# Small results, maxima and conversion words of attention in PSUM, and row sums in four groups

## The chip, the core and the metric

One core of a Trainium2 chip runs the whole program. The metric is the device time of one execution in microseconds (us), as the median of several runs. The engines are TensorE (PE, with its weight loads as PEld), VectorE (DVE), ScalarE (ACT), GpSimd (POOL) and the DMA queues, which SyncE (SP) feeds for the most part. Each engine takes its instructions in the order in which they were written and waits on semaphores for what the others produce.

## What is computed

The reference runs three stages. Attention comes first: queries are averaged in pairs, so that 576 queries meet 1152 keys in each of 4 x 8 heads.

```python
q_pool = q.reshape(B, H, S // factor, factor, D).mean(axis=3)
scores = scale * np.matmul(q_pool, k.transpose(0, 1, 3, 2))
scores = scores - np.max(scores, axis=-1, keepdims=True)
attn = np.exp(scores)
attn = attn / (np.sum(attn, axis=-1, keepdims=True) + 1e-09)
return np.matmul(attn, v).astype(np.float32)
```

The 2304 rows that come out then go through a mixture of 8 experts, where each row takes the expert with the largest gate value, and through one dense feed-forward layer with a softplus. The change touches attention and the gate computation that rides along with it; the expert and feed-forward stages keep their code.

## The kernel before, in words

**Tiling.** `attention` (from L17) handles two heads at once, a pair p, and there are 16 pairs, four in each batch b. A pair has two halves of 288 queries, and a half has nine chunks of 128 keys. A step g is one chunk of one half, so there are 288 steps, counted as `NG`. In step g, `smat` (L168) lets PE compute the scores of the next chunk into a PSUM tile `st` with eight matmuls (L175), `ex` (L176) lets ACT exponentiate them into the SBUF tile `P` (L178), `pv` (L213) lets PE multiply P with v (L218), and `add` (L180) sums P over chunks into tiles `acc`, from which row sums are made.

**Row maxima.** The maximum that is taken off the scores has to be known before `smat` runs on that pair, so a separate pass goes ahead of it. `srow` (L109) computes 384 scores of 128 queries with two matmuls (L118) into a PSUM tile named `sr`, and DVE reduces them to one column (L119). There are 27 such rows for a pair and 432 in all. After the last row of a pair `mfin` (L121) reduces the columns to one maximum (L128, tile `nm`), splits it into two halves of 16 bits (`nh`) and lets PE transpose it into place (L145). For pairs 0 and 1 the split is made by DVE (L130, L131); for the later pairs by two ACT instructions and one on POOL (L135 to L137).

**Row sums.** `GS` (L341) puts the nine chunks in three groups of three. Each group needs two additions, 128 x 576 in f32. They run on POOL (L192), except for chunk 4 of pairs 1 to 13 and chunks 2, 5 and 8 of pair 14, which the table `DVA` (L344) gives to DVE (L190). `rsum` (L194) then sums over the partitions with PE: four matmuls of 288 columns for the first two groups (L203) and four of 144 for the third (L208), each of which the trace shows as two; it stands three steps after the last chunk of its half (`RSD`).

**The gate.** After the last pair of a batch `lstage` (L223) runs once for each half, over batches 0 to 2 with the flag `port`. It divides by the row sums, makes the logits, finds the expert of each row, its gate value and its rank among the rows of that expert, writes the rows of x to DRAM (`xt`, L295) and one-hot rows `OHID` (L332). It is a chain of some 30 short instructions of DVE, with six on POOL among them (L268, L283, L287, L291, L326, L327). The table `LSTEPS` (L338) gives each piece its step after the end of the half.

**Conversions.** Twelve tiles of a later weight arrive as 64-bit words and are turned into f32 by three DVE instructions each (`convert`, L998; L1007, L1008, L1009) while attention runs. The loop from L372 gives each of the three a step of its own, the least busy by an estimate.

**The PSUM tiles `sr`.** The pool `srp` (L36) has three of them, used in turn. Rows of maxima, transposes, row sums and gate matmuls all draw from it, 533 times in attention. A tile can be written again only when the reader of its last use has finished, so PE gets at most three such tiles ahead of the engine that empties them.

**The order.** The loop at L441 writes the instructions out by hand, step by step: `smat` of the next chunk, the copy of a finished half out of PSUM, the exponential, the pieces that tables or `best` (L356) put into this step alternating with rows of maxima, then `pv`, and last the additions. The number of rows by step is set by `rows` (L351).

Of the kernel before, what the change touches and what calls it, by code (L numbers as in the profile page):

```python
# [12 lines left out]
B,H,S,D=4,8,1152,64  # L13
# [3 lines left out]
def attention(ctx,late,tc,I,C,x_dram,LG,gate,fill,early):  # L17
# [12 lines left out]
    accp=ctx.enter_context(tc.tile_pool(name="acc",bufs=4)); ssp=ctx.enter_context(tc.tile_pool(name="ss",bufs=7))  # L30
# [3 lines left out]
    xsp=ctx.enter_context(tc.tile_pool(name="xs",bufs=3))  # L34
# [3 lines left out]
    exp_=srp  # L38
# [82 lines left out]
    def mfin(p,ta=0,tb=9):  # L121
# [37 lines left out]
        return [a]+([a2] if p>=2 else [])+[b,c(0),c(1)]+([d(0),d(1)] if ta==0 else [])  # L159
# [63 lines left out]
    def lstage(b,half,last=False):  # L223
        port=b<B-1; G=nc.gpsimd
# [50 lines left out]
        def ff():  # L275
            V.tensor_reduce(out=T('f',[96,3]),in_=z['eq'],axis=AX.X,op=ALU.min)
# [4 lines left out]
        def ra():  # L281
            V.tensor_reduce(out=T('os',[96,8]),in_=OH.rearrange("p t e -> p e t"),axis=AX.X,op=ALU.add)
            (G if port else V).tensor_tensor(out=C['RS'][:,st+1],in0=C['RS'][:,st],in1=z['os'],op=ALU.add)  # L283
        def ga():
            V.tensor_reduce(out=g,in_=z['ed'],axis=AX.X,op=ALU.add)
        def gb():
            (G if port else V).tensor_scalar(out=g,in0=g,scalar1=1e-9,scalar2=1.0/SX,op0=ALU.add,op1=ALU.mult)  # L287
        def gc():
            V.reciprocal(out=g,in_=g)
        def gd():  # L290
            if last or port: (G if port else V).tensor_tensor(out=z['r'].rearrange("p (t a) h -> p t (a h)",t=3),in0=z['r'].rearrange("p (t a) h -> p t (a h)",t=3),in1=e3(g),op=ALU.mult)  # L291
# [25 lines left out]
        def cm():  # L317
            if last or port: V.tensor_tensor(out=T('cm',[96,3,17]),in0=RK.unsqueeze(2).to_broadcast([96,3,17]),in1=C['iota128'][:96,1:18].unsqueeze(1).to_broadcast([96,3,17]),op=ALU.is_ge)
# [5 lines left out]
        def rp():  # L324
            if port:
                G.tensor_scalar(out=T('rp',[96,3]),in0=RB,scalar1=-128.0,scalar2=None,op0=ALU.mult)  # L326
                G.tensor_tensor(out=z['rp'],in0=z['rp'],in1=RK,op=ALU.add)  # L327
            else: V.scalar_tensor_tensor(out=T('rp',[96,3]),in0=RB,scalar=-128.0,in1=RK,op0=ALU.mult,op1=ALU.add)
        def oi(j):
# [130 lines left out]
    def tail(E,nx):  # L460
# [8 lines left out]
        xs=[xsp.tile([96,512],F32,name="xs") for j in range(3)]  # L469
# [472 lines left out]
def tile_kernel(ctx,tc,I,out):  # L942
    nc=tc.nc
    if True:
      c1=ExitStack(); late=ExitStack(); mst=ExitStack(); P={}
      with tc.manual_schedule():
# [9 lines left out]
        if True:  # L956
# [109 lines left out]
```

## Time and profile before

| what | value |
|---|---|
| median of 3 runs | 1131.71 us (1131.65 to 1132.65) |
| the profiled execution | 1132.7 us, of which the span takes 1130.9 us |
| busy in the span | PE 94%, PEld 62%, DVE 75%, ACT 57%, POOL 43% |
| attention, first to last exponential | from 22.9 us to some 488 us |
| longest groups | DVE L119 225.8 us, ACT L178 185.4 us, PE L218 173.7 us |

Attention is followed by the experts (to about 740 us) and the dense layer. In attention all four engines are busy most of the time, while POOL does little afterwards; a share of the whole span therefore says little, and stretches have to be read one by one. A matmul's busy time is modelled and overlaps with its neighbours'. "Idle before" of an instruction is the engine's idle time ahead of it, and behind the arrow stands the instruction that ended it.

### The profile page before, as it was taken

Reading aid. Unit: us, or ns where it says so; the run is one execution under the profiler, and the core shown is the slowest. Engines: PE = TensorE matmul, PEld = TensorE weight load, DVE = VectorE, ACT = ScalarE, POOL = GpSimd, SP = SyncE. Lnnn points to the kernel's source line nnn. Section 1 sums busy time; section 2 is a strip of 40 time slices with the busy share of each in tenths; the row PEclk is TensorE's granted clock in tenths of the full one; section 3 lists DMA queues with packets and bytes.
Section 4 is the critical chain, followed back from the end, with each engine's and each line's share of the span. In section 5 each row is a group of like instructions: output and inputs, shape, how many; then the busy total and the mean of one; then the engine's idle time right before and its main releaser. Section 6 shows DMA issues by size and latency. Waiting matters only on the chain. (4 is left out here: it accounts for less than half of the span.)

```text
span 1130.9 us, 23702 instructions
## 1 busy us (share of the span) xinstructions
PE 1057.6 (94%) x9423; PEld 706.6 (62%) x9423; DVE 846.1 (75%) x1461; ACT 646.1 (57%) x1136; POOL 491.8 (43%) x414
## 2 busy tenths in 40 slices
PE   5798989999999999998989998999999999999996
PEld 2566756776677666677777777885444444446662
DVE  5867678868886788989798887749867676767762
ACT  5566756776677665657555665646544444444441
POOL 7788867988898885633333222200000100100100
PEclk9999999999999999999999999999999999999999
DMA  9343417441764151426678887731101000000100
GB/s 254 80 106 94 123 47 196 138 123 42 190 148 112 32 154 41 168 86 223 239 254 281 292 274 248 236 112 29 47 1 28 38 1 19 38 1 11 38 10 30
DMA packets 42949, 129.64 MB, mean 115 GB/s; under 512 B 5841, under 2 KB 12881, under 8 KB 40914
## 3 DMA queue, kind: packets, MB, share of 16 engines
q1 hardware_dynamic: 39794, 118.12, 34.9%
q0 software_dynamic: 3040, 9.96, 2.5%
q8 instruction: 76, 1.25, 0.5%
q14 instruction: 39, 0.32, 0.1%
HBM read 108.13 MB, written 20.45 MB: 114 GB/s over the span
## 5 line engine op out<-in xcount | busy, mean ns | idle before, releaser
L119 DVE TENSOR_REDUCE mx<-sr 128x1 f32<-128x384 f32 x432 | 225.8, 550 | 103.9 <-PE sr L118 99.8
L178 ACT ACTIVATE P<-st 128x576 f32<-128x576 f32 x288 | 185.4, 650 | 124.6 <-PE st L175 112.3
L810 POOL DMA_INDIRECT out_dram<-io,CIDS x18 | 21.6, 1198 | 357.0 <-ACT io L808 311.1
L218 PE MATMUL pv<-P,v 128*64 128x288 f32 x1152 | 173.7, 415 | 0.9 <-ACT P L178 0.7
L175 PE MATMUL st<-Q,KB 128*64 128x288 f16 x1152 | 159.2, 289 | 1.9 <-ACT Q L157 1.9
L175 PE MATMUL st<-Q,KA 128*64 128x288 f16 x1152 | 160.0, 290 | 0.0
L118 PE MATMUL sr<-KA,Q 128*64 128x384 f16 x864 | 134.2, 340 | 19.2 <-ACT KA L90 8.3
L192 POOL TENSOR_TENSOR acc<-acc,P 128x576 f32<-128x576 f32 x88 | 124.7, 1417 | 28.8 <-DVE acc L190 22.4
L662 ACT ACTIVATE mhl<-mraw 128x512 f16<-128x512 f32 x160 | 98.1, 625 | 55.3 <-DMA mraw<-in_wm_dram 27.5
L627 PE MATMUL l<-xf,wl 128*128 128x256 f16 (+1 forms) x384 | 125.1, 326 | 0.0
L625 PE MATMUL l<-xf,WIH 128*128 128x256 f16 (+1 forms) x384 | 125.1, 326 | 0.0
L626 PE MATMUL l<-xf,WIH 128*128 128x256 f16 (+1 forms) x384 | 125.1, 326 | 0.0
L667 DVE SCALAR_TENSOR_TENSOR mhl<-mraw,mhl 128x512 f16<-128x512 f32 x140 | 98.7, 725 | 26.2 <-ACT mhl L662 25.5
L192 POOL TENSOR_TENSOR acc<-P 128x576 f32<-128x576 f32 x70 | 100.8, 1440 | 22.1 <-ACT P L178 21.0
L801 PE MATMUL o<-WOH,g 128*128 128x512 f16 x288 | 109.1, 379 | 1.2 <-ACT io L808 0.7
L803 PE MATMUL o<-WOH,g 128*128 128x512 f16 x288 | 109.1, 379 | 0.0
L802 PE MATMUL o<-wl,g 128*128 128x512 f16 x288 | 109.1, 379 | 0.0
L218 PEld LDWEIGHTS pv<-P,v 128*64 128x64 f32 x1152 | 85.9, 139 | 34.8 <-ACT P L178 5.7
L784 ACT ACTIVATE e<-e 128x1024 f32<-128x1024 f32 x36 | 38.0, 1057 | 101.2 <-DVE m L782 101.2
L175 PEld LDWEIGHTS <-KB 128*64 128x64 f16 x1152 | 73.3, 111 | 25.5 <-issue 2.9
L175 PEld LDWEIGHTS <-KA 128*64 128x64 f16 x1152 | 72.9, 111 | 24.0 <-issue 7.1
L626 PE MATMUL l<-hT,mhl 128*128 128x256 f16 x288 | 79.2, 275 | 7.1 <-DVE hT L694 7.1
(256 smaller groups left out, 2240.7 us busy)
## 6 DMA issues: line engine op xcount, KB each, us to landing
mraw<-in_wm_dram SPq DMA_DIRECT2D x80, 512.0 KB, 4.6
kr<-in_k_dram SPq DMA_DIRECT2D x30, 576.0 KB, 9.7
qr<-in_q_dram SPq DMA_DIRECT2D x16, 576.0 KB, 5.9
v<-in_v_dram SPq DMA_DIRECT2D x16, 576.0 KB, 4.3
mraw<-in_w_out_dram SPq DMA_DIRECT2D x16, 512.0 KB, 4.3
stg<-in_w_in_dram SPq DMA_DIRECT2D x12, 512.0 KB, 5.8
y_dram<-w SPq DMA_DIRECT2D x20, 256.0 KB, 4.6
xs_dram<-xs SPq DMA_DIRECT2D x24, 192.0 KB, 2.1
```

The source lines that it names most:

```text
L118: nc.tensor.matmul(sr[64*i:64*i+64,:KW],lhsT=q[:,hh,0,r:r+64],rhs=ka[:,hh,k0:k0+KW],start=True,stop=True)
L119: nc.vector.tensor_reduce(out=MX[p][:,t,kh:kh+1],in_=sr[:,:KW],axis=AX.X,op=ALU.max,negate=True)
L175: nc.tensor.matmul(st[o:o+64,h,:HQ],lhsT=w[:,h,c*128+o:c*128+o+64],rhs=q[:,h,i,qs],start=(i==0),stop=(i==1))
L178: nc.scalar.activation(out=P[g],in_=ST.pop(g)[:,:,:HQ],func=ACTF.Exp,scale=1.0/16)
L192: nc.gpsimd.tensor_tensor(out=A,in0=B_,in1=P[g],op=ALU.add)
L218: nc.tensor.matmul(t[64*h:64*h+64,:HQ],lhsT=V[p][:,c,64*h:64*h+64],rhs=P[g][:,h],start=(c==0),stop=(c==NCH-1))
L625: nc.tensor.matmul(o,lhsT=wh_,rhs=x[0],start=first,stop=False)
L626: nc.tensor.matmul(o,lhsT=wh_,rhs=x[1],start=False,stop=False)
L627: nc.tensor.matmul(o,lhsT=wl_,rhs=x[0],start=False,stop=last)
L801: nc.tensor.matmul(o,lhsT=g[:,0,i,cs],rhs=WOH[:,fc],start=(fc==0),stop=False)
L802: nc.tensor.matmul(o,lhsT=g[:,0,i,cs],rhs=WOL(fc),start=False,stop=False)
L803: nc.tensor.matmul(o,lhsT=g[:,1,i,cs],rhs=WOH[:,fc],start=False,stop=(fc==15))
```

## The change

Row sums are made from four groups of chunks, (0,1), (2,3), (4,5) and (6,7,8). That is five additions for a half instead of six. `DVA` keeps pair 14 alone, so that DVE makes four additions in the whole program instead of 32, and POOL 156 instead of 158. `rsum` has an even number of groups, and so it makes eight matmuls of 288 columns and none of 144. The pool `acc` gets a fifth tile, and `xs` loses its third.

Every pair now splits its maximum on DVE, with `nm` in an `sr` tile. In `lstage` the small intermediates are written to `sr` tiles, the six POOL instructions move to DVE, three reductions are made a second time so that one copy lies in PSUM, and the three one-hot rows are written to one `sr` tile that ACT copies out. The three DVE instructions of a conversion stand directly behind each other, and the first two write an `sr` tile. Three small instructions of the setup go from DVE to POOL. In all the `sr` pool is used 610 times: 17 more for maxima, 12 for conversions and 48 for the gate. `LSTEPS` has new steps.

```diff
-    accp=ctx.enter_context(tc.tile_pool(name="acc",bufs=4)); ssp=ctx.enter_context(tc.tile_pool(name="ss",bufs=7))
+    accp=ctx.enter_context(tc.tile_pool(name="acc",bufs=5)); ssp=ctx.enter_context(tc.tile_pool(name="ss",bufs=7))
...
-    xsp=ctx.enter_context(tc.tile_pool(name="xs",bufs=3))
+    xsp=ctx.enter_context(tc.tile_pool(name="xs",bufs=2))
...
-            st['nm']=smp.tile([128,9],F32,name="nm"); st['nh']=smp.tile([128,9,2],F16,name="nh")
-            nm,nh=st['nm'][:,:n],st['nh'][:,:n]
+
+            st['nh']=smp.tile([128,9,2],F16,name="nh")
+            nm,nh=srp.tile([128,512],F32,name="sr")[:,:n],st['nh'][:,:n]
             nc.vector.tensor_reduce(out=nm,in_=MX[p][:,ta:tb],axis=AX.X,op=ALU.min)
-            if p>=2: return
...
+        def ps(*w): return srp.tile([96,512],F32,name="sr")[:,:w[-1]]
...
             if port:
-                V.tensor_tensor(out=T('d',[96,3,8]),in0=lg,in1=e3(z['m']),op=ALU.is_equal)
-                G.tensor_tensor(out=T('eq',[96,3,8]),in0=z['d'],in1=C['iotaE8'].unsqueeze(1).to_broadcast([96,3,8]),op=ALU.mult)
+
+                w=ps(32); d=w[:,8:32].rearrange("p (t e) -> p t e",t=3)
+                V.tensor_reduce(out=w[:,0:3],in_=lg,axis=AX.X,op=ALU.min)
+                V.tensor_tensor(out=d,in0=lg,in1=e3(w[:,0:3]),op=ALU.is_equal)
+                V.tensor_tensor(out=T('eq',[96,3,8]),in0=d,in1=C['iotaE8'].unsqueeze(1).to_broadcast([96,3,8]),op=ALU.mult)
...
+        def o3():
+            w=srp.tile([96,512],F32,name="sr")[:,:384].rearrange("p (t w) -> p t w",t=3)
+            for j in range(3):
+                V.tensor_scalar(out=w[:,j],in0=C['iota'][:96],scalar1=z['rp'][:,j:j+1],scalar2=C['idc'][:,t0+j:t0+j+1],op0=ALU.is_equal,op1=ALU.mult)
+            nc.scalar.copy(out=C['OHID'][:,t0:t0+3],in_=w)
...
-    NG=NPAIR*18; GS=((0,1,2),(3,4,5),(6,7,8)); GL=((0,1,2,3),(4,5,6),(7,),(8,)); GK=((0,1),(2,3),(4,5),(6,7,8)); ET=238; TS=(1,1,2,4,3); TX=(11,13); RSD=3; LD=2
+    NG=NPAIR*18; GS=((0,1),(2,3),(4,5),(6,7,8)); GL=((0,1,2,3),(4,5,6),(7,),(8,)); GK=((0,1),(2,3),(4,5),(6,7,8)); ET=238; TS=(1,1,2,4,3); TX=(11,13); RSD=3; LD=2
...
-    DVA={**{p:(4,) for p in range(1,14)},14:(2,5,8),15:()}
+    DVA={14:(2,5,8),15:()}
...
-                def b(): nc.vector.tensor_scalar(out=dst,in0=z['s'][:,:,1],scalar1=3,scalar2=0x3FFFFFF8,op0=ALU.logical_shift_left,op1=ALU.bitwise_and)
-                def c(): nc.vector.scalar_tensor_tensor(out=dst,in0=z['s'][:,:,1],scalar=-0x40000000,in1=dst,op0=ALU.bitwise_and,op1=ALU.bitwise_or)
-                def d(): nc.vector.scalar_tensor_tensor(out=dst,in0=z['s'][:,:,0],scalar=29,in1=dst,op0=ALU.logical_shift_right,op1=ALU.bitwise_or)
-                return a,b,c,d
...
+                def c(): nc.vector.scalar_tensor_tensor(out=w(),in0=z['s'][:,:,1],scalar=-0x40000000,in1=w(),op0=ALU.bitwise_and,op1=ALU.bitwise_or)
+                def d(): nc.vector.scalar_tensor_tensor(out=dst,in0=z['s'][:,:,0],scalar=29,in1=w(),op0=ALU.logical_shift_right,op1=ALU.bitwise_or)
+                def bcd(): b(); c(); d()
+                return (a,bcd) if name=="stg" else (a,b,c,d)
...
-                nc.vector.tensor_tensor(out=bias,in0=mf[:,0].unsqueeze(2).to_broadcast([96,24,8]),in1=bb[:,0].unsqueeze(1).to_broadcast([96,24,8]),op=ALU.mult)
+                nc.gpsimd.tensor_tensor(out=bias,in0=mf[:,0].unsqueeze(2).to_broadcast([96,24,8]),in1=bb[:,0].unsqueeze(1).to_broadcast([96,24,8]),op=ALU.mult)
```

On DVE, around the first conversion (`stg` holds the raw words, `w_0_70` the finished tile, `mx` the columns of maxima), there stood before:

```order
L119 TENSOR_REDUCE mx<-sr 128x1 x9
L1007 TENSOR_SCALAR w_0_70<-stg 128x512
L119 TENSOR_REDUCE mx<-sr 128x1 x5
L1008 SCALAR_TENSOR_TENSOR w_0_70<-stg,w_0_70 128x512
L190 TENSOR_TENSOR acc<-P 128x576
L119 TENSOR_REDUCE mx<-sr 128x1 x5
L1009 SCALAR_TENSOR_TENSOR w_0_70<-stg,w_0_70 128x512
```

And now:

```order
L130 TENSOR_SCALAR nh<-sr 128x9
L131 SCALAR_TENSOR_TENSOR nh<-sr,nh 128x9
L119 TENSOR_REDUCE mx<-sr 128x1 x11
L1024 TENSOR_SCALAR sr<-stg 128x512
L1025 SCALAR_TENSOR_TENSOR sr<-stg,sr 128x512
L1026 SCALAR_TENSOR_TENSOR w_0_70<-stg,sr 128x512
L119 TENSOR_REDUCE mx<-sr 128x1 x11
```

The three pieces came together with no row of maxima between them, the addition on DVE is gone, and the split of the maximum is here.

On DVE, in the first half of the gate of batch 0 (`LG` logits, `m` their best, `d` and `eq` the search for the expert, `OH` its one-hot rows), there stood before:

```order
L267 TENSOR_TENSOR d<-LG,m 96x24
L119 TENSOR_REDUCE mx<-sr 128x1
L1009 SCALAR_TENSOR_TENSOR w_1_71<-stg,w_1_71 128x512
L119 TENSOR_REDUCE mx<-sr 128x1 x3
L285 TENSOR_REDUCE gate<-ed 96x3
L276 TENSOR_REDUCE f<-eq 96x3
L119 TENSOR_REDUCE mx<-sr 128x1
L278 TENSOR_TENSOR OH<-cc,f 96x24
```

And now:

```order
L264 TENSOR_REDUCE sr<-LG 96x3
L265 TENSOR_TENSOR sr<-LG,sr 96x24
L266 TENSOR_TENSOR eq<-sr,cc 96x24
L119 TENSOR_REDUCE mx<-sr 128x1 x3
L275 TENSOR_REDUCE sr<-eq 96x3
L277 TENSOR_TENSOR OH<-cc,sr 96x24
L119 TENSOR_REDUCE mx<-sr 128x1
L286 TENSOR_REDUCE sr<-ed 96x3
L288 TENSOR_SCALAR gate<-sr 96x3
```

The product `eq` came over from POOL, `OH` stands directly behind its minimum, and each short result passes through an `sr` tile of its own.

On PE, at the first row sum (`one_198` is a column of ones), there stood before:

```order
L118 MATMUL sr<-KA_190,Q_196 64x384
L203 MATMUL sr<-acc,one_198 32x288 x4
L208 MATMUL sr<-acc,one_198 32x144 x4
L118 LDWEIGHTS Q_196
L118 MATMUL sr<-KA_190,Q_196 64x384
```

And now:

```order
L118 MATMUL sr<-KA_190,Q_196 64x384
L197 MATMUL sr<-acc,one_198 32x288 x8
L118 LDWEIGHTS Q_196
L118 MATMUL sr<-KA_190,Q_196 64x384
L118 LDWEIGHTS Q_196
```

Its place is the same, and its second part is twice as wide.

## Rows read from the trace of the kernel before

**Rows 1.** Stretches: length, busy us (instructions) of PE, PEld, DVE, ACT, POOL, clock, DMA
```profile
75.00:100.00 25.00, 22.39 (x273) 15.08 (x275) 18.04 (x30) 18.55 (x36) 24.00 (x19) 1.00 0.66 167
100.00:125.00 25.00, 23.15 (x266) 16.70 (x264) 18.29 (x33) 15.29 (x30) 19.89 (x16) 0.93 0.23 70
150.00:175.00 25.00, 21.75 (x240) 13.71 (x241) 18.03 (x42) 14.61 (x30) 16.94 (x21) 0.93 0.32 94
...
262.62:310.69 48.07, 44.44 (x521) 29.85 (x521) 38.23 (x84) 31.72 (x63) 38.50 (x40) 1.00 0.53 135
310.69:361.74 51.05, 50.83 (x640) 37.79 (x638) 38.36 (x70) 38.84 (x75) 45.50 (x37) 1.00 0.55 143
```

**Rows 2.** Waits of PE in attention, 0 to 495 us: total, times, longest
```profile
PE sr L118 <- DVE mx L119: 8.2, 15, 1.4
PE sr L145 <- DVE nh L131: 6.2, 3, 3.7
PE sr L203 <- DVE mx L119: 3.8, 2, 2.7
PE sr L208 <- POOL acc L192: 3.7, 3, 1.3
PE sr L310 <- DVE mx L119: 2.4, 3, 0.8
```

**Rows 3.** Waits of POOL in attention, same stretch
```profile
POOL acc L192 <- DVE acc L190: 22.4, 16, 3.0
POOL rp L326 <- DVE RB L323: 9.2, 6, 2.0
```

**Rows 4.** Timeline at 51 us, split of pair 1's maximum: start, us, instruction, idle before
```profile
53.57 2.54 DVE L131 SCALAR_TENSOR_TENSOR nh<-nm,nh 128x9 f16<-128x9 f32 x1
...
56.17 0.27 PE L145 MATMUL sr<-ident,nh 128*2 128x128 f16 x2 [3.69 <-DVE nh L131]
```

**Rows 5.** Timeline from 147 us, a conversion in the gate of batch 0
```profile
147.48 4.55 DVE L1009 SCALAR_TENSOR_TENSOR w<-stg,w 128x512 int32<-128x512 int32 x1
...
152.65 0.69 PE L203 MATMUL sr<-acc,one 128*32 128x288 f32 x8 [2.67 <-DVE mx L119]
...
154.83 2.13 PE L218 MATMUL pv<-P,v 128*64 128x288 f32 x8
```

**Rows 6.** Groups of instructions by form: count, busy us, mean ns, idle before
```profile
L1008 DVE SCALAR_TENSOR_TENSOR w<-stg,w 128x512 int32<-128x512 int32 x12 | 15.7, 1307 | 0.1
L1008 DVE SCALAR_TENSOR_TENSOR w<-mraw,w 128x512 int32<-128x512 int32 x20 | 13.8, 691 | 0.6
L190 DVE TENSOR_TENSOR acc<-P 128x576 f32<-128x576 f32 x26 | 29.8, 1146 | 0.0
L302 DVE TENSOR_TENSOR xs<-sr,r 96x512 f32<-96x512 f32 x21 | 14.2, 678 | 0.1
L332 DVE TENSOR_SCALAR OHID<-cc,rp 96x128 f16<-96x128 f32 x18 | 13.9, 797 | 0.0
L247 DVE TENSOR_SCALAR r<-sr 96x24 f32<-96x24 f32 x6 | 1.0, 172 | 0.3 <-PE sr L245 0.2
L267 DVE TENSOR_TENSOR d<-LG,m 96x24 f32<-96x24 f32 x6 | 1.0, 168 | 0.0
L131 DVE SCALAR_TENSOR_TENSOR nh<-nm,nh 128x5 f16<-128x5 f32 x1 | 0.2, 171 | 0.0
L192 POOL TENSOR_TENSOR acc<-acc,P 128x576 f32<-128x576 f32 x86 | 121.6, 1414 | 27.6 <-DVE acc L190 22.4 <-ACT P L178 1.6
```

**Rows 7.** Timeline at 353 us: a row sum, then PE's next matmul
```profile
353.24 0.69 PE L203 MATMUL sr<-acc,one 128*32 128x288 f32 x8
...
353.75 0.43 PE L208 MATMUL sr<-acc,one 128*32 128x144 f32 x8
...
354.11 0.35 PE L118 MATMUL sr<-KA,Q 128*64 128x384 f16 x2
```

**Rows 8.** DMA issues of the page: count, KB each, us to landing
```profile
xs_dram<-xs SPq DMA_DIRECT2D x24, 192.0 KB, 2.1
```

More of the change, by code (lines that the diff above doesn't have):

```diff
@@ L37, in attention @@
     pvp=ctx.enter_context(tc.tile_pool(name="pv",bufs=1,space=PSUM))
-    exp_=srp
+    exp_=srp; C['Z']['srp']=srp
     NS=3
@@ L281, in ra @@
         def ra():
+            if port: z['os']=ps(8)
             V.tensor_reduce(out=T('os',[96,8]),in_=OH.rearrange("p t e -> p e t"),axis=AX.X,op=ALU.add)
[L283 removed]
+            V.tensor_tensor(out=C['RS'][:,st+1],in0=C['RS'][:,st],in1=z['os'],op=ALU.add)
         def ga():
[L285 removed]
+            if port: z['g']=ps(3)
+            V.tensor_reduce(out=T('g',[96,3]) if port else g,in_=z['ed'],axis=AX.X,op=ALU.add)
         def gb():
[L287 removed]
+            V.tensor_scalar(out=g,in0=z['g'] if port else g,scalar1=1e-9,scalar2=1.0/SX,op0=ALU.add,op1=ALU.mult)
         def gc():
[L289 removed]
+            if port: z['g']=ps(3)
+            V.reciprocal(out=z['g'] if port else g,in_=g)
         def gd():
[L291 removed]
+            if last or port: V.tensor_tensor(out=z['r'].rearrange("p (t a) h -> p t (a h)",t=3),in0=z['r'].rearrange("p (t a) h -> p t (a h)",t=3),in1=e3(z['g'] if port else g),op=ALU.mult)
             else:
@@ L317, in cm @@
         def cm():
-            if last or port: V.tensor_tensor(out=T('cm',[96,3,17]),in0=RK.unsqueeze(2).to_broadcast([96,3,17]),in1=C['iota128'][:96,1:18].unsqueeze(1).to_broadcast([96,3,17]),op=ALU.is_ge)
+            rk_=RK
+            if port:
+                rk_=ps(3); V.tensor_reduce(out=rk_,in_=z['rt'],axis=AX.X,op=ALU.add)
+            if last or port: V.tensor_tensor(out=T('cm',[96,3,17]),in0=rk_.unsqueeze(2).to_broadcast([96,3,17]),in1=C['iota128'][:96,1:18].unsqueeze(1).to_broadcast([96,3,17]),op=ALU.is_ge)
             else:
@@ L324, in rp @@
         def rp():
+            rb_=RB
             if port:
-                G.tensor_scalar(out=T('rp',[96,3]),in0=RB,scalar1=-128.0,scalar2=None,op0=ALU.mult)
-                G.tensor_tensor(out=z['rp'],in0=z['rp'],in1=RK,op=ALU.add)
-            else: V.scalar_tensor_tensor(out=T('rp',[96,3]),in0=RB,scalar=-128.0,in1=RK,op0=ALU.mult,op1=ALU.add)
+                rb_=ps(3); V.tensor_reduce(out=rb_,in_=z['cm'],axis=AX.X,op=ALU.add)
+            V.scalar_tensor_tensor(out=T('rp',[96,3]),in0=rb_,scalar=-128.0,in1=RK,op0=ALU.mult,op1=ALU.add)
         def oi(j):
@@ L373, in attention @@
         lo=max(lo,last+1); hi=max(hi,lo+3); first=None
-        for n,(f,c) in enumerate(zip(fs,(0.35,0.6,0.6))):
-            g=best(lo,hi-2+n); lo=g+1
+        for n,(f,c) in enumerate(zip(fs,(1.85,))):
+            g=best(lo,hi); lo=g+1
             if first is None: first=g
@@ L439, in row @@
             p=done//SRN-1; MF=mfin(p,5 if p==0 else 0); MF[0]()
-            pend.extend([(g+d,f) for d,f in zip((1,1,1,1,1) if p<2 else (1,4,4,4,4,4),MF[1:])])
+            pend.extend([(g+d,f) for d,f in zip((1,1,1,1,1) if p==1 else (3,3,3,3,2),MF[1:])])
     for g in range(NG+1):
@@ L468, in tail @@
         E.step(TS[0]); L['pe1'](); E.step(TS[1]); L['pe2']()
-        xs=[xsp.tile([96,512],F32,name="xs") for j in range(3)]
+        xs=[xsp.tile([96,512],F32,name="xs") for j in range(2)]+[accp.tile([128,2,HQ],F32,name="acc").rearrange("p a b -> p (a b)")[:96,:512]]
         for j in range(3):
@@ L994, in yz @@
                 return z
-            C['setup']=setup0; C['later']=((20,setup1),(24,setup2),(27,setup5),(44,setup3),(46,setup4))+tuple((50+8*k,yz(k)) for k in range(4*YW//512))
+            C['Z']={}; C['setup']=setup0; C['later']=((20,setup1),(24,setup2),(27,setup5),(44,setup3),(46,setup4))+tuple((50+8*k,yz(k)) for k in range(4*YW//512))
             fill=[]
```

25 lines of the change are left out of this document (14 added, 11 removed).

## The prediction

> **What bounds the kernel now.** The change lies in attention, so I first split that stretch by time and looked at which engine is full. Between 310 and 361 us PE is busy for 50.83 of 51.05 us while DVE has 38.36 and POOL 45.50: there PE sets the pace, and 36 steps take 1.42 us each [rows 1]. Other stretches are not like that. From 262 to 310 us, where a gate runs, PE is busy for 44.44 of 48.07 us; from 100 to 125 and from 150 to 175 us it has 23.15 and 21.75 of 25 us, and its granted clock averages 0.93 [rows 1]. So the gain of any relief for DVE or POOL is the idle time of PE, and its price is new work on PE.
>
> Next come PE's waits by their ends. Five groups hold almost all that DVE and POOL cause: 8.2, 6.2, 3.8, 3.7 and 2.4 us [rows 2], 24.3 us together, in 26 waits. The long ones have one pattern. The second part of the split of pair 1's maximum takes 2.54 us for nine columns, and PE waits 3.69 us for it [rows 4]; the same instruction on five columns took 171 ns [rows 6]. One conversion instruction lasts 4.55 us, and PE then waits 2.67 us at the row sum [rows 5], although the same operation takes 691 ns on average once attention is over [rows 6]. What differs is POOL, which runs long instructions back to back beside the slow ones. In the rows, slow DVE instructions have two SBUF inputs (L131, L1008, L190) or are scalar operations from SBUF to SBUF (L332, 797 ns for 128 columns), while L302 with one input in PSUM has a mean of 678 ns for 512 columns over its 21 [rows 6].
>
> This also hits POOL, which waits 22.4 us for DVE's additions and 9.2 us in the gate [rows 3]. Such waits delay its additions, hence the row sums that wait on POOL (3.7 us) [rows 2].
>
> The Trainium skill (SBUF — State Buffer, section "Who interferes with whom") says that a DVE instruction with two SBUF inputs, or in a mode that uses two ports, excludes a GpSimd instruction that reads SBUF for its whole length, and that one with at most one SBUF input outside that mode does not. The trace agrees: 171 ns against 2.54 us for the same kind of split.
>
> **The change part by part.** All is set against the profiled execution, 1132.7 us with a span of 1130.9 us; the median shown is 1131.71 us, 1.0 us less, and I apply the difference to that.
>
> (a) Splits of the maximum. With `nm` in PSUM none of the three instructions has two inputs in SBUF any more, so three of some 0.17 us [rows 6] stand behind the last row. The three waits of 6.2 us [rows 2] shrink to some 0.3 us each: a gain of 5.3 us, between 4 and 6.2. For the other 14 pairs DVE gets two more short instructions, and two of ACT and one of POOL go; none of them is on PE's path in the rows.
>
> (b) DVE behind with rows, which PE feels as waits for an `sr` tile: 8.2 + 3.8 + 2.4 = 14.4 us in 20 waits [rows 2]. DVE loses 28 additions at 1.15 us, 32 us [rows 6]. Of each conversion the two instructions with two inputs fall from some 1.31 to some 0.69 us, 12 x 2 x 0.62 = 15 us [rows 6]. The one-hot rows, 18 at 797 ns, come to no more than the 678 ns of a four times wider form [rows 6], at least 2 us. Against this come about ten more short instructions for each of six gates, at 0.17 us, 10 us [rows 6]. DVE is thus relieved of some 39 us, while it now idles for a quarter of a clean stretch. I take three quarters of the 14.4 us, 10.8 us; the bounds are 5 and 14.4, since a conversion of 3 x 0.68 = 2.0 us in one piece can still hold up a row.
>
> (c) Row sums that wait for POOL: 3.7 us in three waits [rows 2]. POOL no longer waits for DVE's additions or inside the gate, but its own additions are 156 against 158 at 1.41 us [rows 6]. Around 100 us POOL is full by itself (24.00 of 25 us [rows 1]), so one of the three stays. Gain 2.5 us, between 0 and 3.7.
>
> (d) Granted clock. After the wait at 152 us eight matmuls of L218 take 2.13 us [rows 5] in the stretch with a mean clock of 0.93; the lower of the two levels, 1.2 GHz, was granted for a moment there after PE had idled. Two stretches at 0.93 cost about 25 x 0.07 = 1.75 us each [rows 1]. If the waits before them go, so do these. I take 2.5 of 3.5 us, the bounds being 0 and 3.5.
>
> (e) The fourth group costs PE. The first half of a row sum runs 0.51 us (353.24 to 353.75) and the narrow one 0.36 us (353.75 to 354.11) [rows 7]. Two wide ones are 0.15 us longer, in 30 halves 4.5 us, all on the path where PE is full. Nothing hides it.
>
> (f) 77 more `sr` tiles in the turn of three. A tile that DVE alone writes and reads leaves PE one fewer to run ahead with. No row shows such a tile. What DVE's lag costs now is 14.4 us over 533 tiles, 0.03 us each; a wait when it does occur costs 8.2/15 = 0.55 us [rows 2]. I take 0.05 us each, 3.9 us, near the lower row because most tiles are held for two short instructions; ends 0 and 0.55 us. A new wait hides in it: DVE may now have to wait for ACT, when the tile's last reader was a copy of ACT, and behind DVE stand the rows that PE needs emptied.
>
> (g) Three setup instructions of 192 columns on POOL, by the 1.41 us for 576 columns [rows 6] some 1.5 us, at about 103 us, right behind the stretch in which POOL is full. The slack of three steps before a row sum covers most; I take 0.5 us, between 0 and 1.5.
>
> A third `xs` tile less costs nothing: the three are written over three steps of 1.42 us, and a store lands in 2.1 us [rows 8]. The fifth `acc` tile is what the additions of the next half need, because two groups are open before the row sum frees the old ones.
>
> A rule that speaks against the change: the Trainium skill (VectorE: DVE Perf Modes, section on the errata) gives a fixed cost of 120 cycles for a VectorE instruction from PSUM and 58 for one from SBUF, an estimate of 65 ns more at 0.96 GHz. The trace does not show it here: 172 ns from PSUM (L247) and 168 ns from SBUF (L267) for the same 96 x 24 [rows 6]. By the rule some 100 instructions would add 6 to 7 us to DVE, and by the ratio of (b) under 1 us to the time.
>
> Sum: 5.3 + 10.8 + 2.5 + 2.5 = 21.1 us gained; 4.5 + 3.9 + 0.5 = 8.9 us paid; 12.2 us remain. 1131.7 - 12.2 = **1119.5 us**. The later stages take over what attention gives, since PE starts them in the same order.
>
> **The rivals.**
>
> *Turn of three (slower).* PE becomes tied to DVE through the added tiles. It decides the sign at (21.1 - 4.5 - 0.5) / 77 = 0.21 us for each tile. At 0.35 us, 27 us, the result is 1131.7 - 21.1 + 5.0 + 27 = 1143 us. For it: 14 tiles instead of 6 in one gate, some of them next to each other without a row between. Against: DVE waits often for PE today, and each short result is used up at once.
>
> *POOL takes over the bound (smaller gain).* POOL has 45.50 of 51.05 us in the clean stretch and 24.00 of 25 us near 75 us [rows 1], and its work hardly shrinks. Then half of (a) and of (b) and all of (c) go again: 2.7 + 5.4 + 2.5 - 8.9 = 1.7 us, or 1130 us.
>
> *DVE still waits for POOL when it writes PSUM (slower).* The rows show PSUM as an input, never as an output of DVE. Then a conversion stays at 3.6 us but in one piece; if each holds PE for 1.7 us, as part of the 2.67 us did, 12 of them cost 20 us, and only the removed additions (say 8 us) help: 1131.7 + 20 + 8.9 - 8 = 1153 us. L302, with one input in PSUM, speaks against it.
>
> *All waits go (larger gain).* 6.2 + 14.4 + 3.7 + 3.5 = 27.8 us less 4.5 us is 23.3 us: 1108 us.
>
> **How the numbers follow.** Forecast 0.54 (its own range 1111 to 1127 us), larger gain 0.11, POOL 0.16, turn of three 0.13, waits that stay 0.06. About what a measurement here can tell from no change is 0.2%, 2.3 us. POOL's case is split between faster (0.08) and the same (0.08), a little of the turn-of-three's lower end lies within 0.2% (0.02), the rest of it and the last rival are slower (0.17). Faster: 0.54 + 0.11 + 0.08 = 0.73. The range of 8 in 10 takes in the larger gain and POOL's case and leaves the two slower ones out: 1107 to 1132 us.
>
> **What would show it.** Right: L131 at some 0.17 us throughout; the conversions at 0.7 us a piece with little spread; no wait of PE of over 2 us behind DVE; POOL with no wait on DVE's additions in pairs 1 to 13; a granted clock of 1.00 from 100 to 175 us; row sums with two parts of 0.51 us. Wrong: PE waits for DVE on `sr` of 20 us or more in total, with the L118 waits more than 15 in number; DVE waits for ACT at the first write of an `sr` tile; a conversion of over 3 us; POOL full at 95% in attention with PE's waits at POOL grown.

## The result: slower, 1141.9 us against 1132.6 us

Measured side by side on one chip, the changed kernel takes 1141.89 us in the median and the kernel before 1132.55 us; the ratio is 1.0074 with a 95% interval from 1.0055 to 1.0092. The forecast was 1119.5 us and faster, with a range that ended at 1132 us. So the sign is wrong, and the outcome lies beside the rival "turn of three" (1143 us). One execution of the changed kernel had a mean granted clock of 0.659 and took 1571.66 us; the ratio leaves it out, and the profile of the changed kernel that is read here (after_again) is another one, with a clock of 0.995. The changed kernel was timed again with the first experiments: 1140.41 against 1131.94 us.

The page of the changed kernel, busy time by engine:

```profile
span 1140.8 us, 23704 instructions
PE 1067.2 (94%) x9423; PEld 705.4 (62%) x9423; DVE 792.4 (69%) x1506; ACT 644.1 (56%) x1114; POOL 472.2 (41%) x365
```

PE still has 94% and DVE fell from 75% to 69%. So DVE was relieved, and the time went up all the same. What DVE did with the relief stands in its own waits. Of before, then of after:

```profile
DVE mx L119 <- PE sr L118: 98.1, 126, 4.3
```

```profile
DVE mx L119 <- PE sr L118: 139.0, 155, 4.4
```

DVE waits 41 us more for rows from PE. The question is therefore what holds PE. Its waits in attention (total, times, longest), to be held against [rows 2]:

```profile
...
PE sr L301 <- ACT OHID L343: 6.9, 6, 1.2
PE sr L118 <- DVE mx L119: 4.0, 9, 0.7
PE sr L118 <- DVE w L1026: 2.9, 6, 1.5
PE sr L301 <- DVE lp L247: 2.1, 3, 0.7
PE sr L229 <- DVE mx L119: 2.0, 3, 0.7
PE sr L312 <- DVE gate L288: 1.9, 3, 0.6
...
PE sr L197 <- POOL acc L186: 1.6, 2, 1.3
```

The old waits shrank as planned: the 6.2 us at the split are gone, 8.2 us are 4.0, 3.7 us at POOL are 1.6. In their place stand new waits for `sr` tiles. Behind the first row is the one-hot tile `OHID`; behind L1026 a conversion; L229, L301 and L312 are PE's own pieces of the gate (logits, transposes, ranks), which wait for a tile that DVE has not done with. The stretch of [rows 1] in which batch 1's gate runs (steps 144 to 170, 262.62 to 310.69 us before) reads now, with length, then busy us of PE, PEld, DVE, ACT, POOL, clock, DMA:

```profile
257.85:308.63 50.78, 45.24 (x521) 29.46 (x519) 32.37 (x94) 31.97 (x63) 34.72 (x26) 1.00 0.48 129
```

The same 521 matmuls take 50.78 instead of 48.07 us; PE idles for 5.5 us instead of 3.6, while DVE is busy 5.9 us less. The same columns for all of attention, first before, then after:

```profile
22.87:487.74 464.87, 437.07 (x5218) 305.68 (x5216) 360.66 (x681) 310.94 (x595) 372.28 (x313) 0.99 0.41 113
```

```profile
23.06:495.18 472.12, 444.64 (x5219) 303.60 (x5217) 305.71 (x726) 309.51 (x573) 352.45 (x264) 1.00 0.41 111
```

DVE is busy 55 us less, but PE idles for 27.5 us where it idled for 27.8 us: as much waiting came in as went out. What is left is that PE itself is busy 7.6 us longer, about what the fourth group adds to it (7.2 us, under (e) below).

By stretches, in us between the starts of the exponentials in the traces (the last row runs to the end of the last one; no_gate and the others are the experiments below):

| steps | before | after | no_gate | no_grp | only_mf | gate_sbuf | three_groups |
|---|---|---|---|---|---|---|---|
| 0-53, pairs 0 to 2 | 95.7 | 86.4 | 86.9 | 85.6 | 90.3 | 86.3 | 86.9 |
| three gates (72-98, 144-170, 216-242) | 147.9 | 153.3 | 140.0 | 152.0 | 147.5 | 138.7 | 138.9 |
| between gates (99-143, 171-215) | 130.4 | 135.4 | 135.4 | 133.2 | 133.1 | 135.4 | 133.2 |
| pair 14 (252-269) | 23.9 | 28.1 | 27.9 | 28.5 | 23.7 | 27.6 | 23.7 |
| all of attention | 464.9 | 472.1 | 459.2 | 467.9 | 462.0 | 456.9 | 451.3 |

The expected gain is there in pairs 0 to 2 (9.3 us). It is lost in the gates (5.4 us), between them (5.0), in pair 14 (4.2) and in some 2 us elsewhere, 1.7 of them in steps 54 to 71 (27.8 to 29.5), where a conversion stands in one piece. From the end of attention to the end of the kernel the profiles of all kernels here take 641.7 to 649.2 us, in no order that goes with attention's end, so one profile does not carry differences of some 3 us in the total. Below, the totals go by the timed ratios and the places by the table.

### The profile page after: what moved, and what is told of

Same layout as the page of the kernel before. It is cut to its first block, busy times and chain, and to the rows that moved or that the text cites. A ratio compares the mean times of both kernels' runs of the same rounds, so it can differ in the third digit from the quotient of the medians.

```text
span 1569.6 us, 23704 instructions
## 1 busy us (share of the span) xinstructions
PE 1533.6 (98%) x9423; PEld 834.5 (53%) x9423; DVE 811.6 (52%) x1506; ACT 657.6 (42%) x1114; POOL 471.6 (30%) x365
## 3 DMA queue, kind: packets, MB, share of 16 engines
q8 instruction: 76, 1.25, 0.3%
## 5 line engine op out<-in xcount | busy, mean ns | idle before, releaser
L212 PE MATMUL pv<-P,v 128*64 128x288 f32 x1152 | 242.0, 552 | 0.0
L186 POOL TENSOR_TENSOR acc<-P 128x576 f32<-128x576 f32 x124 | 174.4, 1407 | 224.0 <-ACT P L172 194.3
L169 PE MATMUL st<-Q,KB 128*64 128x288 f16 x1152 | 207.7, 365 | 2.0 <-ACT Q L151 2.0
L169 PE MATMUL st<-Q,KA 128*64 128x288 f16 x1152 | 209.3, 369 | 0.0
L118 PE MATMUL sr<-KA,Q 128*64 128x384 f16 x864 | 165.4, 433 | 14.3 <-ACT KA L90 8.2
L639 PE MATMUL l<-xf,WIH 128*128 128x256 f16 (+1 forms) x384 | 166.2, 433 | 0.0
L640 PE MATMUL l<-xf,wl 128*128 128x256 f16 (+1 forms) x384 | 165.5, 431 | 0.0
L638 PE MATMUL l<-xf,WIH 128*128 128x256 f16 (+1 forms) x384 | 165.3, 430 | 0.0
L816 PE MATMUL o<-WOH,g 128*128 128x512 f16 x288 | 148.0, 514 | 0.0
L815 PE MATMUL o<-wl,g 128*128 128x512 f16 x288 | 147.9, 514 | 0.0
L814 PE MATMUL o<-WOH,g 128*128 128x512 f16 x288 | 147.8, 513 | 0.0
L789 DVE TENSOR_SCALAR m<-l 128x512 f32<-128x512 f32 x72 | 49.7, 690 | 142.4 <-ACT e L788 142.3
L788 ACT ACTIVATE e<-l 128x512 f32<-128x512 f32 x72 | 42.9, 597 | 174.2 <-PE l L640 174.2
L638 PE MATMUL l<-xx,mhl 128*128 128x256 f16 x288 | 100.0, 347 | 0.7 <-ACT ye L745 0.7
```

The costliest lines, as they stand in the source:

```text
L118: nc.tensor.matmul(sr[64*i:64*i+64,:KW],lhsT=q[:,hh,0,r:r+64],rhs=ka[:,hh,k0:k0+KW],start=True,stop=True)
L169: nc.tensor.matmul(st[o:o+64,h,:HQ],lhsT=w[:,h,c*128+o:c*128+o+64],rhs=q[:,h,i,qs],start=(i==0),stop=(i==1))
L186: nc.gpsimd.tensor_tensor(out=A,in0=B_,in1=P[g],op=ALU.add)
L212: nc.tensor.matmul(t[64*h:64*h+64,:HQ],lhsT=V[p][:,c,64*h:64*h+64],rhs=P[g][:,h],start=(c==0),stop=(c==NCH-1))
L638: nc.tensor.matmul(o,lhsT=wh_,rhs=x[0],start=first,stop=False)
L639: nc.tensor.matmul(o,lhsT=wh_,rhs=x[1],start=False,stop=False)
```

## The experiments

**The parts, one undone at a time.** The change was timed again beside three kernels with one part back as before. Theory A: the turn of three `sr` tiles ties PE to DVE, above all in the gate. Theory B: the fourth group of the row sums is what costs.

> The changed kernel once more, for a trace at full clock. Theory A (turn of three: 77 more sr tiles tie PE to DVE): PE's waits on sr tiles behind DVE total over 20 us, more than 15 of them at L118. Theory B (four groups: more columns on PE, and the additions of the next half wait for the row sum to free an acc tile): PE's waits behind DVE fall under 10 us, row sums take 2 x 0.51 us, POOL waits for PE at L197 for over 10 us in total. Both: some 8 us slower than before.

Measured: 1140.41 us, ratio 1.0070 (1.0041 to 1.0098). Neither list of signs came in whole: PE waits 18.4 us behind DVE for `sr` tiles (22.6 us before), 15 times at L118 for rows and conversions, and POOL's additions wait 2.7 us at L197.

The gate as before, all else as changed (cut):

```diff
-        def ps(*w): return srp.tile([96,512],F32,name="sr")[:,:w[-1]]
+        port=b<B-1; G=nc.gpsimd
...
-            nc.scalar.copy(out=C['OHID'][:,t0:t0+3],in_=w)
...
+                G.tensor_scalar(out=T('rp',[96,3]),in0=RB,scalar1=-128.0,scalar2=None,op0=ALU.mult)
+                G.tensor_tensor(out=z['rp'],in0=z['rp'],in1=RK,op=ALU.add)
```

> The change without its gate: lstage and its steps as before (POOL instructions and SBUF intermediates back), all else changed; 48 of the 77 added sr tiles go. Theory A: the gates are most of the loss, so 5 us or more come back (ratio under 1.003). Theory B: nothing comes back, some 2 us are lost because DVE and POOL hold each other up again (ratio 1.008 to 1.010).

Measured: 1125.99 us, ratio 0.9941 (0.9924 to 0.9958). The gate's part costs 14.4 us; without it the change is faster than before.

```diff
-GS=((0,1),(2,3),(4,5),(6,7,8))
-    DVA={14:(2,5,8),15:()}
+GS=((0,1,2),(3,4,5),(6,7,8))
+    DVA={**{p:(4,) for p in range(1,14)},14:(2,5,8),15:()}
```

> The change without its row sums: three groups of three chunks and DVE's additions as before, all else changed. Theory A: only the 4.5 us of wider row sums come back, so it stays slower than before by some 4 us (ratio 1.003). Theory B: all is won back and more, 5 to 10 us faster than before (ratio 0.993), since the relief of DVE and POOL is then free of its price.

Measured: 1137.76 us, ratio 1.0046 (1.0029 to 1.0062): 2.7 us back, so B does not explain the loss. In its trace PE is busy 7.8 us less in attention than in the changed kernel, but idles 3.7 us more.

```diff
-                return (a,bcd) if name=="stg" else (a,b,c,d)
+                return a,b,c,d
```

(with the three pieces of a conversion in SBUF and at steps of their own, as before)

> The change without its conversions: three steps each and results straight to SBUF as before, all else changed; 12 of the 77 added sr tiles go. Theory A: a piece of 2.0 us that holds a tile of the three is the worst kind, 3 us or more come back (ratio 1.005 or less). Theory B: nothing comes back, 2 to 4 us are lost (ratio 1.009 to 1.011).

Measured: 1142.44 us, ratio 1.0083 (1.0060 to 1.0105), within the uncertainty of the changed kernel. Two effects offset, counted as in the table: this kernel has 23.5 us in pair 14 (28.1 in the change) and 27.9 in steps 54 to 71 (29.5), but 138.0 us between the gates (135.4) and 87.2 us in pairs 0 to 2 (86.4). So neither theory's range was met: the early conversions gain and lose by their place, and those of pair 14 lose.

**What in the gate costs.** Theory C is A for the gate's 48 tiles; D says the work that moved to DVE costs, E the closer steps. Three changes of the gate alone:

```diff
-        def ps(*w): return srp.tile([96,512],F32,name="sr")[:,:w[-1]]
+        def ps(w):
+            z['n']+=1
+            return lsp.tile([96,w],F32,name=f"s{z['n']}")
...
-            nc.scalar.copy(out=C['OHID'][:,t0:t0+3],in_=w)
+            for j in range(3): oi(j)()
```

> The changed kernel, but the short results of the gate lie in SBUF tiles of their own and the one-hot rows are written straight to OHID by three DVE instructions; the other instructions of the gate, the move from POOL to DVE and the steps stay. 48 sr tiles fewer. Theory C (the gate's cost is the turn of three sr tiles: 14.4 us over 48 tiles, 0.3 us each): most of the 14.4 us comes back, 1126 to 1130 us. Rival D (the cost is the work itself, six POOL instructions and four second reductions now on DVE): nothing comes back, 1139 to 1142 us. Rival E (the new steps, closer together, cost it): also 1139 to 1142 us.

Measured: 1127.65 us, ratio 0.9957 (0.9931 to 0.9983). That is theory C's range; D and E expected nothing back.

The second hunk alone:

> The changed kernel, but the three one-hot rows go straight to OHID in SBUF, at the same step, with no sr tile and no copy by ACT (6 of the 48 sr tiles fewer). Theory C with equal tiles at 0.3 us: 6 x 0.3 = 1.8 us back, 1138.6 us. Theory C with unequal tiles (the tile that ACT has to read is held longest; six waits of PE at the transposes behind it, 6.9 us, and 2.1 us more beside them): 1132 to 1134 us. Rivals D and E: no change, 1140 us.

Measured: 1134.42 us, ratio 1.0007 (0.9988 to 1.0026). Six tiles carry about half of the gate's price: the three gates, counted as in the table, take 145.8 instead of 153.3 us, 1.25 us a tile. The trace of the changed kernel shows why (timeline: start, us, instruction, idle before and what ended it):

```profile
275.45 1.29 DVE L342 TENSOR_SCALAR sr<-cc,rp 96x128 f32<-96x128 f32 x3
...
276.78 0.47 ACT L343 CAST OHID<-sr 96x384 f16<-96x384 f32 x1 [1.25 <-DVE sr L342]
...
277.31 0.64 PE L301 MATMUL sr<-ident,xu 128*96 128x128 f32 x4 [1.23 <-ACT OHID L343]
```

The tile is held for 1.8 us by two engines in a row, and PE, whose next transposes want the same place in the turn, stands for 1.23 us. ACT stands too, for 1.25 us, in front of its next work.

```diff
-    LSTEPS="... fo 9 gab 10 ra 11 rk 11 gcd 12 rt 12 rr 13 cm 13 xt0 14 cr 14 rp 15 xt1 15 o3 16 xt2 17".split()
+    LSTEPS="... gab 10 fo 10 gcd 12 rk 13 ra 13 rt 14 rr 14 cm 15 xt0 15 cr 16 rp 16 xt1 16 xt2 17 o3 19".split()
```

> The changed kernel with the pieces of the gate at the steps of the kernel before; the sr tiles stay, all 48. Rival E (the new steps cost it): 1127 to 1130 us. Theory C: the tiles stand further apart with rows between, so a part comes back, 1134 to 1140 us. Rival D: no change, 1140 us.

Measured: 1143.50 us, ratio 1.0087 (1.0055 to 1.0119). Nothing comes back, so E falls; the waits only change place (6.9 us in three waits of L118, up to 2.3 us). Theory C's range was missed too: tiles that stand further apart cost no less.

**The turn, or PSUM itself?** gate_sbuf takes away the turn and the place of the results at once. The first attempt to part them put 30 results into unused columns of the `pv` tile:

```diff
+            if w!=32 and 'f' in z and PV: return list(PV.values())[-1][:96,320:320+w]
```

> As gate_sbuf, but 30 of the 42 short results (gate values, counts, ranks, bases) lie in PSUM again, in columns 320 and up of the pv tile, which PV leaves free: PSUM without a turn in sr. Theory C (the turn is what costs): as gate_sbuf, 1126 to 1129 us. Rival F (DVE's writing and reading of PSUM beside PE is what costs): 30/42 of the 6.8 us that lie between gate_o3 and gate_sbuf come back, 1131 to 1133 us.

Measured: 1138.81 us, ratio 1.0054 (1.0031 to 1.0076), which neither theory gave. Its waits of PE in attention:

```profile
PE pv L212 <- DVE cm L325: 5.9, 6, 1.4
PE pv L212 <- DVE RS L285: 4.7, 6, 1.1
PE pv L212 <- DVE rp L335: 3.2, 6, 0.8
...
PE sr L118 <- DVE mx L119: 1.9, 4, 0.7
```

The `sr` waits of the gate are gone, but 13.8 us of new ones stand at the P x v matmuls: PE was tied to DVE's chain through the `pv` tile, though the columns are apart. The Trainium skill (PSUM — Partial Sum Buffer, section "PSUM bank collisions raise a hardware error") says that two engines must be kept apart on a bank and a group of 32 partitions, whatever the columns. The waits fit a program that keeps to this: 18 waits, all for DVE's instructions on the spare columns. Whether its semaphores go by bank or by tile, and what the chip does without them, no run shows. So the run does not part the theories; it only shows a price of the same kind at another tile. A pair of kernels goes further. Both are gate_sbuf; at each of the 42 places one has DVE write zeros into a fresh `sr` tile, which nobody reads, the other into an SBUF tile:

```diff
             z['n']+=1
+            V.memset(srp.tile([128,512],F32,name="sr")[:96,:w],0.0)
             return lsp.tile([96,w],F32,name=f"s{z['n']}")
```

> As gate_sbuf (all short results of the gate in SBUF), but at each of the 42 places where the change takes an sr tile one is taken, and DVE writes a few zeros into it and nothing reads it: the turn of three alone, with a short hold. Theory C (the turn costs, some 0.16 us for each of these 42): 1132 to 1135 us, as gate_o3 (1134.4). Rival F (DVE's work on the results in PSUM costs, not the turn): as gate_ctl.

> The control of gate_ring: the same 42 writes of zeros by DVE, into an SBUF tile, and no sr tile taken. Both theories: gate_sbuf (1127.7) and at most 2 us more for 42 short DVE instructions, 1127 to 1130 us.

Measured: gate_ring 1136.91 us, ratio 1.0039 (1.0016 to 1.0062); gate_ctl 1126.60 us, ratio 0.9961 (0.9938 to 0.9985). The first is a little above theory C's range, and F, which expected the two to be equal, falls. The difference of the ratios, 0.0078, is 8.8 us for 42 tiles, 0.21 us each, with the results in SBUF in both. The change's own 42 short tiles come out somewhat cheaper: gate_o3 against gate_sbuf is 0.0050 in the ratios, 5.7 us or 0.13 us each, and 7.1 us or 0.17 us each in the three gates of the traces (145.8 and 138.7 us). Steps 144 to 170 of gate_ring, of gate_ctl and, with no such writes, of gate_sbuf:

```profile
257.40:306.14 48.74, 45.14 (x521) 29.95 (x519) 37.90 (x108) 31.33 (x60) 34.68 (x26) 1.00 0.50 130
```

```profile
253.84:299.84 46.00, 44.97 (x521) 30.03 (x519) 38.70 (x108) 31.23 (x61) 34.81 (x26) 1.00 0.51 140
```

```profile
252.65:298.62 45.97, 44.96 (x521) 30.03 (x519) 36.28 (x94) 31.25 (x60) 34.86 (x26) 1.00 0.52 140
```

All have the same matmuls. 14 more DVE writes cost nothing (46.00 against 45.97 us), the same writes in `sr` 2.7 us, and nearly all of it is idle time of PE (3.60 against 1.03 us). The waits of PE from 90 to 460 us, of gate_ring and of gate_ctl:

```profile
PE sr L118 <- DVE mx L119: 5.1, 10, 1.0
PE sr L118 <- DVE w L1025: 2.9, 6, 1.5
PE sr L303 <- DVE lp L249: 2.2, 3, 0.7
...
PE sr L231 <- DVE sr L222: 1.3, 2, 0.7
PE sr L314 <- DVE s L288: 1.1, 3, 0.4
```

```profile
PE sr L118 <- DVE w L1025: 2.9, 6, 1.5
PE sr L118 <- DVE mx L119: 1.5, 3, 0.5
...
PE sr L197 <- DVE xs L306: 1.0, 3, 0.3
```

All rows of the two lists come to 18.0 and 9.9 us, so 8.1 us of the difference are such waits. Only a few of them name the write itself (`sr` L222). Most are for a row or for a gate result: a tile that DVE alone uses takes one of three places, and PE reaches its limit one tile earlier. A ring of another length, and DVE results in a PSUM tile that PE does not use, were not tried.

Rival D falls with gate_ctl and gate_sbuf too: both have all the moved work on DVE and give the time back.

**The parts that were thought to gain.** The splits of the maximum alone:

> The kernel before with the splits of the maximum of all pairs on DVE through an sr tile (17 tiles more) and nothing else. If the splits and the clock behind them give what pairs 0 to 2 gained in every variant (18.8 + 18.1 + 12.7 + 15.3 + 13.7 + 17.1 us against 14.9 + 14.7 + 13.9 + 14.6 + 13.5 + 14.8 us, 9.3 us) and the 17 tiles cost nothing: 1121 to 1124 us. If a tile costs 0.3 us each here too: 1126 to 1129 us. If the gain came from the setup on POOL: 1129 to 1133 us.

Measured: 1132.34 us, ratio 0.9994 (0.9975 to 1.0012). The number is that of the third expectation (setup on POOL), but none of the three holds in whole. 5.4 us in pairs 0 to 2 are there (95.7 to 90.3), and 2.7 us are paid back between the gates (130.4 to 133.1), where PE was full and five pairs run, half a microsecond for each. Whether that is their `sr` tile or the other steps of their transposes was not parted; the run also has the change's fifth `acc` tile and its two `xs` tiles. Most of what pairs 0 to 2 gain beyond this (90.3 to 86.4) lies in steps 45 to 53, and is taken up under (g) below.

**A version that beats both.** Early conversions through `sr`, late ones as before, with the gate and the three groups of the kernel before (cut, against the changed kernel):

```diff
-//n-1,convert(i))); i+=1
+//n-1,convert(i,old=p>=14))); i+=1
...
-                return (a,bcd) if name=="stg" else (a,b,c,d)
+                return (a,bcd) if name=="stg" and not old else (a,b,c,d)
```

> The kernel before with the splits of the maximum in PSUM, the setup on POOL and the conversions of pairs 2 to 11 in one piece through sr; the gate, the three groups with DVE's additions and the six conversions of pair 14 stay as before. Expected from the single parts: 1126.0 (gate as before) less 2.7 (three groups) less 4 us (pair 14: halves of 14.4 and 13.6 us against 12.4 and 11.1 us) = 1119 to 1122 us. If the parts don't add up because DVE's additions hold up the rows again in pairs 1 to 13: 1124 to 1128 us.

Measured: 1124.54 us, ratio 0.9923 (0.9893 to 0.9953). The sum of the single parts was missed, and the second range was met; that DVE's additions are the reason was not tested. With the gate of gate_sbuf added:

> The splits of the maximum, the gate on DVE with its short results in SBUF (as gate_sbuf), setup on POOL, conversions of pairs 2 to 11 in one piece, three groups with DVE's additions and the conversions of pair 14 as before. If the parts add up: 1124.5 (mf_conv) less 4 to 5 us that its gates take longer than those of gate_sbuf (48.3 + 2 x 46.8 against 3 x 46.0 us) = 1119 to 1121 us. If DVE, with the additions and the whole gate, falls behind: 1124 to 1128 us.

Measured: 1122.77 us, ratio 0.9905 (0.9883 to 0.9927), between the two ranges. And with the fourth group:

> As three_groups, but with the four groups of the change and no additions on DVE in pairs 1 to 13. From gate_sbuf (1127.7) less 4 us for the conversions of pair 14: 1123 to 1125 us; slower than three_groups by the 2.7 us of the fourth group, unless DVE's additions hold it up there.

Measured: 1123.50 us, ratio 0.9914 (0.9895 to 0.9934). Both are faster than either kernel; three_groups by 9.1 us over before in the medians, and its attention by 13.6 us (451.3 against 464.9). The two differ by less than their intervals: the fourth group's price and that of DVE's additions are about equal here. four_groups against gate_sbuf (1127.65 us) gives the price of pair 14's conversions in one piece: 4.2 us in the medians, and 4.4 us in pair 14 of the traces (27.6 to 23.2 us). Steps 144 to 170 of three_groups, where PE idles 1.75 us instead of 3.6:

```profile
252.17:298.23 46.06, 44.31 (x521) 30.12 (x519) 39.64 (x97) 31.22 (x60) 34.10 (x27) 1.00 0.51 138
```

## Why the prediction was wrong, step by step

**(f), the 77 `sr` tiles, failed.** The prediction took 0.05 us each, 3.9 us, "near the lower row because most tiles are held for two short instructions". The runs showed 0.13 to 0.17 us for the gate's 42 short tiles (gate_o3 against gate_sbuf), 0.21 us for one that is held for a single write (gate_ring against gate_ctl) and 1.25 us for the tile that DVE fills and ACT empties. The gate's 48 come to 12.8 us by the ratios of gate_sbuf and to 14.6 us in its three gates, some 0.3 us each, where 2.4 us were taken for all of them: an error of 10 to 12 us, against a forecast gain of 12.2 us. The error was the choice of the row. The lower one, 14.4 us over 533 tiles, averages over tiles that PE itself fills. An added one takes a place from PE and gives it back only when DVE, which has rows to work off as well, has come to it; that is read from the waits. That the added tiles stand close together is not the reason by itself, since gate_steps won nothing. The bound that the prediction named as deciding, 0.21 us, was passed by the average of the gate's tiles. The mechanism was seen, as a rival; its chance was set at 0.13.

**A second part of (f), the conversions**, was covered as "12 tiles". Against no_conv, a conversion in one piece gains 2.6 us between the gates and costs 1.6 us in steps 54 to 71; in pair 14, where six stand in 13 steps, they cost 4.2 us. Waits for them name 1.8 us of that; the rest is time in which PE counts as busy, and its cause stays open. The longest such wait in pair 14:

```profile
462.83 0.94 PE L197 MATMUL sr<-acc,one 128*32 128x288 f32 x12 [0.94 <-DVE w L1026]
```

**(a) was right, its size partly by luck.** L131 has 174 ns for nine columns, beside POOL's work, and pairs 0 to 2 gain 5.4 us in only_mf; 5.3 us were forecast. But in only_mf the stretch from 25 to 50 us also went from a granted clock of 0.93 to 1.00, by the prediction's own sum some 1.75 us that belong to (d). That the other 14 pairs' splits cost nothing was wrong (2.7 us between the gates). The forms in the changed kernel's attention (count, busy us, mean ns), beside [rows 6]:

```profile
L1025 DVE SCALAR_TENSOR_TENSOR sr<-stg,sr 128x512 int32<-128x512 int32 x12 | 8.3, 695 | 0.4
L1026 DVE SCALAR_TENSOR_TENSOR w<-stg,sr 128x512 int32<-128x512 int32 x12 | 8.2, 687 | 0.4
...
L342 DVE TENSOR_SCALAR sr<-cc,rp 96x128 f32<-96x128 f32 x18 | 7.3, 406 | 0.4
...
L131 DVE SCALAR_TENSOR_TENSOR nh<-sr,nh 128x9 f16<-128x9 f32 x15 | 2.6, 174 | 0.5
```

**(b): the relief came, its worth did not.** The conversions are at 0.69 us a piece, the one-hot rows at 406 instead of 797 ns. DVE is busy 55 us less in attention, where 39 us were worked out, and 41 us of that it now waits longer for PE. Of the three groups of waits at 14.4 us, L118 has 4.0 us left and the row sum (L203, now L197) 0.6 us; the rank matmuls (L310, now L312) still have 1.9 us, now behind the gate value. So 7.9 us went, where 10.8 us were taken; in their place stand 6.9 us at the one-hot tile, 2.9 us at conversions and 2.1 + 2.0 us in the gate. The rule that the prediction named against the change would, by the ratio of (b), 10.8 to 39, have cost some 1.8 us and not under 1; nothing in the sum hung on it. And part of the relief was to be had without PSUM: in gate_sbuf the one-hot rows go straight to SBUF, three steps earlier than before, and take less than the 406 ns into PSUM:

```profile
L338 DVE TENSOR_SCALAR OHID<-cc,rp 96x128 f16<-96x128 f32 x18 | 5.1, 334 | 0.0
```

In the gates themselves, the changed kernel without the new gate (no_gate) shows the relief: 147.9 to 140.0 us.

**(c)** 3.7 us became 1.6 us, in two waits; 2.5 us of gain were forecast, 2.1 came. POOL has no wait for DVE's additions left in pairs 1 to 13. Its waits are now for ACT, where the same row had 22.6 us before:

```profile
POOL acc L186 <- ACT P L172: 84.9, 43, 5.7
```

**(d) was undersized.** The stretches that had a clock of 0.93 in [rows 1] are at 1.00, and a third one, which the prediction did not count, as well. The stretch from 25 to 50 us before, and the same of after:

```profile
25.00:50.00 25.00, 22.45 (x240) 16.33 (x238) 18.41 (x36) 13.42 (x25) 17.76 (x14) 0.93 0.47 110
```

```profile
25.00:50.00 25.00, 24.15 (x287) 17.53 (x285) 19.80 (x44) 16.74 (x30) 18.54 (x15) 1.00 0.54 127
```

By the prediction's own sum that is 3 x 1.75 = 5.3 us of lower clock gone, where 2.5 us were taken. The first of the three lies in pairs 0 to 2 and is part of the 9.3 us gained there.

**(e) was undersized.** A row sum in the changed kernel:

```profile
299.89 1.18 PE L197 MATMUL sr<-acc,one 128*32 128x288 f32 x16
301.00 0.35 PE L118 MATMUL sr<-KA,Q 128*64 128x384 f16 x2
```

It takes 1.11 us until PE's next matmul, against 0.87 us in [rows 7]: 0.24 us a half, not 0.15, and 7.2 us for 30; most of the halves of either trace have just these times. The prediction had taken the time of one wide part twice, 1.02 us; two of them take 1.11. Since DVE's additions also cost time, giving the group back with them saves only 2.7 us (no_grp).

**(g) had the wrong sign, as far as the runs show.** No wait of PE names the setup work on POOL. But steps 45 to 53, in which it stands, take 17.1 us before and 17.3 us in only_mf, both with the setup on DVE, and 14.8 to 15.3 us in every variant that has it on POOL: some 2 us gained where 0.5 us were to be paid. On DVE the three instructions take 1.15, 1.55 and 1.32 us in a row, and rows wait behind them; on POOL they take 0.51 to 0.58 us. The second one, before and after:

```profile
105.58 1.55 DVE L982 TENSOR_TENSOR LG<-mf,bb 96x192 f32<-96x192 f32 x1
```

```profile
102.09 0.51 POOL L995 TENSOR_TENSOR LG<-mf,bb 96x192 f32<-96x192 f32 x1
```

In only_mf the stretch from 100 to 125 us still has a clock of 0.93, so one of the three stretches of (d) may belong here too. No run moved the setup alone.

**The rivals.** "Turn of three" is what happened, at 0.3 us a tile in the gate instead of the 0.35 us for all 77 that it was worked out with. That the total meets its 1143 us so closely is partly chance: the gate, the splits and pair 14 come to some 21 us (14.4 + 2.7 + 4.2) where it had 27, and (d), (e) and (g) were off as well. "POOL takes over the bound" did not: between two gates (steps 171 to 206 of the changed kernel) POOL has 45.83 us, as before [rows 1], and PE is full:

```profile
308.63:361.77 53.14, 52.58 (x640) 38.46 (x638) 34.42 (x72) 38.33 (x69) 45.83 (x35) 1.00 0.51 137
```

"DVE still waits for POOL when it writes PSUM" is refuted by the forms above. "All waits go" failed with (f).

**The signs named beforehand.** Right ones seen: L131 at 0.17 us, conversions at 0.7 us, no wait of over 2 us behind DVE, a clock of 1.00 from 100 to 175 us. The two parts of a row sum took 1.11 us, not twice 0.51. The wrong ones were badly set: 20 us of waits for DVE, which the kernel before already has (22.6 us), and over 15 at L118. The L118 waits were 15 in number with the conversions, the total behind DVE was 18.4 us and lay at other lines, and the largest group stood behind ACT, while the sign for ACT looked at DVE waiting for it; PE was the one that did.

## What to carry to other kernels

A place in a small ring of PSUM tiles that PE also uses has a price of its own, even if the tile is held for one short instruction: price it by the wait of the engine that fills the ring, in the stretch where the tile is taken, not by an average over the program. Taking an engine's stalls away is worth only what the bounding engine waits for it: DVE's SBUF version of the gate is busy 3.9 us longer in steps 144 to 170 (36.28 against 32.37 us) and 4.8 us faster. So move a temporary to PSUM only where the bounding engine waits for it now, as for the splits of the first pairs.

## What was not expected of the hardware

The lengths of DVE's instructions with an operand in PSUM hardly spread beside a busy POOL: the 36 instructions of the 12 conversions take 682 to 697 ns each, where those of L1008 took 693 to 1805 ns before. A tile of PSUM that two engines use had them wait for each other even on disjoint columns (18 waits, 13.8 us in gate_pv), by the program's semaphores. An SBUF-to-SBUF form is not slow by itself: the one-hot rows have 797 ns in the kernel before and 334 ns in gate_sbuf, with the same operands at another step; what POOL does beside them was not varied.
